# Retention attention and gated convolution: steps of 256 tokens with two tokens per partition instead of steps of 128

## Chip, cores, metric

One core of one Trainium2 chip. The metric is the device time of one execution in microseconds (us). Times are medians of all runs of a kernel. A run counts as slow when it is over 1.5% above the fastest of the same kernel; ratios leave such runs out. On one core this goes by time alone. "Span" is the profiled execution on the core alone, some 2 us shorter than its time.

## The reference

```python
# q, k, v: (B=8, H=8, S=576, D=64) float32; d_model = H*D = 512; conv kernel of 5
scores = q @ k.T / sqrt(D)
gamma  = 1 - 2 ** (-5 - arange(H))
ret    = scores * where(i >= j, gamma ** (i - j), 0)     # causal decay, per head
x      = (ret @ v).transpose(0, 2, 1, 3).reshape(B, S, 512)
gate   = sigmoid(sum_k conv_w[k] * x_padded[:, k:k+S])   # causal depthwise convolution
out    = (gate * (x @ w_val)) @ w_out
```

The decay factors into gamma^i for q and gamma^-j for k. So attention runs in chunks: scores inside a chunk with a 0/1 mask, and a 64x64 state per head for all earlier tokens.

## The kernel before

A step is 128 tokens of one batch (four steps, then one rest step of 64 tokens for two batches together). GpSimd (POOL) casts and scales, TensorE (PE) transposes, VectorE (DVE) and ScalarE (ACT) take the results out of PSUM. The convolution is 160 matmuls of 32x32 tiles in one piece of "fill" work, which stands between attention steps along with the two matrix products.

```python
def load(s):                                  # 256 B per run: one token of one head
    eng.dma_start(out=dst, in_=src[b, :, c*P:(c+1)*P, :].rearrange("h p d -> p h d"))

def scores(s):                                # 64x128 tiles
    for hh in range(2):
        for hp in range(HP):
            nc.tensor.matmul(sc[:, hp, :], lhsT=kt[sl, hp, :], rhs=qt[sl, hp, :], ...)

def state(s):                                 # summed in PSUM, 128x128 matmuls, half of it unused
    for hp in range(HP):
        nc.tensor.matmul(sp[:, hp, :], lhsT=kb[:, 2*hp:2*hp+2, :], rhs=vb[:, 2*hp:2*hp+2, :],
                         start=(c == 0 and hp == 0), ...)
    # ... diagonal blocks copied to w by ScalarE

def attn_out(s):
    # ... o (one PSUM bank): 8 matmuls of 128x64 tiles, 4 from the state
    nc.scalar.copy(xt[:, :, bb, PAD + c*P:PAD + (c+1)*P], o)

for s in range(NS):
    load(s + 4); cast(s + 2); transp(s + 1)
    scores(s); state(s)
    # two pieces of fill (conv, val or outp)
    attn_out(s)
    # one or two pieces of fill
    # at the end of a batch: push_block(...) puts conv, four val, m outp on the list of fill
```

Of the kernel before, what the change touches and what calls it, by code (L numbers as in the profile page):

```python
# [14 lines left out]
F32 = mybir.dt.float32  # L15
# [10 lines left out]

@with_exitstack
def kernel(
# [10 lines left out]
    nc = tc.nc  # L39
# [3 lines left out]
    NC = S // P  # L43
    REM = S - NC * P
# [4 lines left out]
    assert D == 64 and DM == H * D and 2 * REM == P and B % 2 == 0  # L49
# [7 lines left out]
    ld = ctx.enter_context(tc.tile_pool(name="ld", bufs=6))  # L57
    cs = ctx.enter_context(tc.tile_pool(name="cs", bufs=4))
    at = ctx.enter_context(tc.tile_pool(name="at", bufs=3))
    xp = ctx.enter_context(tc.tile_pool(name="xp", bufs=2))  # L60
# [5 lines left out]
    opp = ctx.enter_context(tc.tile_pool(name="opp", bufs=1, space=PS))  # L66
    stp = ctx.enter_context(tc.tile_pool(name="stp", bufs=1, space=PS))
    glp = ctx.enter_context(tc.tile_pool(name="glp", bufs=4, space=PS))


    ident = cst.tile([P, P], BF16)
    make_identity(nc, ident)
    pos_i = cst.tile([P, NC + 1], I32)
    nc.gpsimd.iota(pos_i, pattern=[[P, NC + 1]], base=0, channel_multiplier=1)
    pos = cst.tile([P, NC + 1], F32)
    nc.vector.tensor_copy(pos, pos_i)
    nc.vector.tensor_scalar(pos[REM:P, NC:NC + 1], pos[REM:P, NC:NC + 1], -float(REM), None,
                            op0=ALU.add)
    fq = cst.tile([P, NC + 1, H], F32)
    fk = cst.tile([P, NC + 1, H], F32)  # L80
    for h in range(H):
        nc.scalar.activation(fq[:, :, h], pos, AF.Exp, scale=lng[h])
        nc.scalar.activation(fk[:, :, h], pos, AF.Exp, scale=-lng[h])
    nc.vector.tensor_scalar_mul(fq, fq, scale)

    mask_c = cst.tile([P, P], F32)
    nc.vector.memset(mask_c, 1.0)
    nc.gpsimd.affine_select(mask_c, mask_c, pattern=[[1, P]], base=0, channel_multiplier=-1,
                            compare_op=ALU.is_ge, fill=0.0)
    mask_r = cst.tile([P, P], F32)  # L90
    nc.vector.memset(mask_r, 0.0)
    for half in range(2):
        sl = slice(half * REM, (half + 1) * REM)
        nc.vector.tensor_copy(mask_r[sl, sl], mask_c[sl, sl])


    NW = 4
    wst = []
    for i in range(NW):
        w = cst.tile([P, HP, P], BF16, tag=f"wst{i}")  # L100
        nc.vector.memset(w, 0.0)
        wst.append(w)
# [9 lines left out]
    diag = cst.tile([P, 2, KC, DT, Q], BF16)  # L112
    wval = cst.tile([P, DT, NQ, P], BF16)
    wout = cst.tile([P, NQ, DM], BF16)

    def load_weights():
# [4 lines left out]
        wtmp = cst.tile([P, DT, DM], BF16)  # L121
        nc.gpsimd.dma_start(out=wtmp, in_=moe_w_val.rearrange("(do di) dp -> di do dp", di=P))
        for do in range(DT):
            nc.vector.tensor_copy(wval[:, do].rearrange("p r (c x) -> p r c x", x=Q),
                                  wtmp[:, do].rearrange("p (c r x) -> p r c x", r=NQ, x=Q))
# [5 lines left out]
        nc.vector.tensor_copy(cwh, cw)  # L131
        nc.vector.tensor_tensor(cwl, cw, cwh, op=ALU.subtract)
        nc.vector.tensor_tensor(idr, ident[:, 0:Q], ident[:, Q:2 * Q], op=ALU.add)
        for i in range(2, NQ):
            nc.vector.tensor_tensor(idr, idr, ident[:, i * Q:(i + 1) * Q], op=ALU.add)
        shp = [P, KC * DT, Q]
        for p2, w in ((0, cwh), (1, cwl)):
            nc.vector.tensor_tensor(
                diag[:, p2].rearrange("p k c x -> p (k c) x"),
                idr.unsqueeze(1).to_broadcast(shp),  # L140
                w.rearrange("p k c -> p (k c)").unsqueeze(2).to_broadcast(shp), op=ALU.mult)


    steps = []
    for u in range(B // 2):
        for bb in range(2):
            for c in range(NC):
                steps.append((u, bb, c))
        steps.append((u, None, NC))

    st = {}

    def load(s):
        u, bb, c = steps[s]
        r = st.setdefault(s, {})
        qf = ld.tile([P, H, D], F32)
        kf = ld.tile([P, H, D], F32)
        vf = ld.tile([P, H, D], F32)
        if bb is None:
            for x in range(2):  # L160
                b = 2 * u + x
                sl = slice(x * REM, (x + 1) * REM)
                for dst, src, eng in ((qf, q, nc.sync), (kf, k, nc.sync), (vf, v, nc.sync)):
                    eng.dma_start(out=dst[sl], in_=src[b, :, NC * P:S, :].rearrange("h p d -> p h d"))
        else:
            b = 2 * u + bb
            for dst, src, eng in ((qf, q, nc.sync), (kf, k, nc.sync), (vf, v, nc.sync)):
                eng.dma_start(out=dst, in_=src[b, :, c * P:(c + 1) * P, :].rearrange("h p d -> p h d"))
        r.update(qf=qf, kf=kf, vf=vf)

    def cast(s):
        c = steps[s][2]
        r = st[s]
        qb = cs.tile([P, H, D], BF16)
        kb = cs.tile([P, H, D], BF16)
        nc.gpsimd.tensor_tensor(qb, r["qf"], fq[:, c, :].unsqueeze(2).to_broadcast([P, H, D]), op=ALU.mult)  # L176
        nc.gpsimd.tensor_tensor(kb, r["kf"], fk[:, c, :].unsqueeze(2).to_broadcast([P, H, D]), op=ALU.mult)  # L177
        vb = cs.tile([P, H, D], BF16)
        nc.gpsimd.tensor_copy(vb, r["vf"])  # L179
        r.update(qb=qb, kb=kb, vb=vb)  # L180

    def transp(s):
        r = st[s]
        tp = glp.tile([P, 2, HP, P], BF16, tag="gps", name="tp")
        for n, src in ((0, r["qb"]), (1, r["kb"])):
            for hp in range(HP):
                nc.tensor.transpose(tp[:, n, hp, :], src[:, 2 * hp:2 * hp + 2, :].rearrange("p a d -> p (a d)"), ident)  # L187
        qt = at.tile([P, HP, P], BF16)
        kt = at.tile([P, HP, P], BF16)
        nc.vector.tensor_copy(qt, tp[:, 0])  # L190
        nc.scalar.copy(kt, tp[:, 1])  # L191
        r.update(qt=qt, kt=kt)

    def scores(s):
        u, bb, c = steps[s]
        r = st[s]
        mk = mask_r if bb is None else mask_c
        r["am"] = []
        for hh in range(2):
            sl = slice(hh * D, (hh + 1) * D)  # L200
            sc = scp.tile([P, HP, P], F32)
            for hp in range(HP):
                nc.tensor.matmul(sc[:, hp, :], lhsT=r["kt"][sl, hp, :], rhs=r["qt"][sl, hp, :],  # L203
                                 start=(hp == 0), stop=True, skip_group_check=True)
            am = at.tile([P, HP, P], BF16, tag=f"am{hh}")
            nc.vector.tensor_tensor(am, sc, mk.unsqueeze(1).to_broadcast([P, HP, P]), op=ALU.mult)  # L206
            r["am"].append(am)

    wcur = {}
    wcount = [0]  # L210
    stbank = {}

    def state(s):
        u, bb, c = steps[s]
        if bb is None:
            return
        r = st[s]
        if c == 0:
            stbank[0] = stp.tile([P, HP, P], F32, name="sts")
        sp = stbank[0]  # L220
        for hp in range(HP):
            nc.tensor.matmul(sp[:, hp, :], lhsT=r["kb"][:, 2 * hp:2 * hp + 2, :].rearrange("p a d -> p (a d)"),  # L222
                             rhs=r["vb"][:, 2 * hp:2 * hp + 2, :].rearrange("p a d -> p (a d)"),
                             start=(c == 0 and hp == 0), stop=True, skip_group_check=True)

        w = wst[2 + bb] if c == NC - 1 else wst[c % 2]
        for hh in range(2):
            sl = slice(hh * D, (hh + 1) * D)
            nc.scalar.copy(w[sl, :, hh * D:(hh + 1) * D], sp[sl, :, hh * D:(hh + 1) * D])  # L229
        wcur[(u, bb, c + 1)] = w  # L230
# [3 lines left out]
    def attn_out(s):  # L234
        u, bb, c = steps[s]
        r = st[s]
        if u not in xts:
            xt = xp.tile([P, DT, 2, PAD + S], BF16, name="xt")
            nc.gpsimd.memset(xt[:, :, :, 0:PAD], 0.0)
            xts[u] = xt  # L240
        xt = xts[u]
        o = opp.tile([P, HP, P], F32)
        for hp in range(HP):
            for hh in range(2):
                sl = slice(hh * D, (hh + 1) * D)
                nc.tensor.matmul(o[sl, hp, :], lhsT=r["vb"][:, 2 * hp + hh, :], rhs=r["am"][hh][:, hp, :],  # L246
                                 start=(hp == 0), stop=True, skip_group_check=True)
        if c > 0:
            for hp in range(HP):
                if bb is None:  # L250
                    for x in range(2):
                        cl = slice(x * REM, (x + 1) * REM)
                        nc.tensor.matmul(o[:, hp, cl], lhsT=wcur[(u, x, NC)][:, hp, :], rhs=r["qt"][:, hp, cl],
                                         start=False, stop=True, skip_group_check=True)
# [143 lines left out]
```

## Time and profile before

| | before |
|---|---|
| time, runs beside the changed kernel | 221.05 us (220.55 to 222.78, 4 runs) |
| span of the profiled run | 217.4 us |
| PE busy | 174.5 us |
| PE idle | 42.9 us |
| first scores | 23.10 us |
| first convolution starts; runs through from | 39.12 us; 41.83 us |
| PE idle after 41.83 us | 21.4 us |

PE's busy time comes from the page, idle is span less busy, and the last row is the sum of the windows' lengths less PE's busy time in them. The start, on PE's timeline (37 of the first convolution's 160 matmuls run ahead of 41.83):

```profile
23.10 0.62 PE L203 MATMUL sc<-qt,kt 64*128 64x128 bf16 x8
...
39.12 1.04 PE L288 MATMUL cps<-xt,diag 32*32 32x512 bf16 x15
...
40.62 0.63 PE L288 MATMUL cps<-xt,diag 32*32 32x512 bf16 x22
41.83 2.40 PE L288 MATMUL cps<-xt,diag 32*32 32x512 bf16 x123 [0.57 <-ACT kt L191]
```

Next is the page's list of DMA queues of the kernel before (packets, MB, share of 16 engines' time):

```profile
q1 hardware_dynamic: 117760, 37.76, 79.1%
...
q8 instruction: 27, 0.44, 0.9%
```

The last is PE's waits in the kernel before (us in total, times, longest):

```profile
PE cps L288 <- issue: 5.6, 3, 2.8
...
PE vps L303 <- ACT gt L295: 2.4, 3, 1.6
...
PE cps L288 <- ACT kt L191: 1.2, 4, 0.6
PE cps L288 <- ACT xt L261: 0.7, 2, 0.3
```

Waits are given as us in total, times, longest; "issue" means that PE waits for nothing that the profile shows.

### The profile page before, as it was taken

The page shows a single profiled execution, that of the slowest core. Times are in us where ns is not written, and L with a number is a line of the kernel's source. Part 1 is how long each engine was busy: PE and PEld are TensorE (multiplying, and loading weights), DVE is VectorE, ACT ScalarE, POOL GpSimd, SP SyncE. Part 2 cuts the span into 40 slices and gives each one's busy share as a digit, 9 for nine tenths or more (in the row PEclk, how much of TensorE's full clock was granted, in tenths as well). Part 3 has the DMA queues.
Part 4 walks back from the last instruction along what each step waited for, and adds up shares of the span by engine and source line. Part 5 has one row for each costly group of instructions (what it writes and reads, how often), then busy time and mean ns, then how long its engine had stood idle before and what let it go on. Part 6 is the DMA issues. An engine that isn't in the chain of part 4 may idle for free.

```text
span 217.4 us, 8277 instructions
## 1 busy us (share of the span) xinstructions
PE 174.5 (80%) x3532; PEld 110.5 (51%) x3552; DVE 92.4 (43%) x182; ACT 106.7 (49%) x242; POOL 98.7 (45%) x125
## 2 busy tenths in 40 slices
PE   0003899899949949999999879699898999999950
PEld 0002466455735528665664566356644866576640
DVE  2037434364604415555535255356363454535310
ACT  2021263556803625746863547448457474666321
POOL 7007997471445415708444854355656463200000
PEclk9999999999997996999999999999999999999997
DMA  6999999953998399669899998699989996130122
GB/s 119 177 214 217 217 221 201 183 104 102 275 205 191 106 238 202 135 155 234 245 238 192 218 306 179 156 195 250 289 192 199 236 262 134 58 141 34 69 100 50
DMA packets 121540, 39.33 MB, mean 181 GB/s; under 512 B 115872, under 2 KB 116896, under 8 KB 121504
## 3 DMA queue, kind: packets, MB, share of 16 engines
q1 hardware_dynamic: 117760, 37.76, 79.1%
q0 software_dynamic: 1104, 1.05, 3.0%
q8 instruction: 27, 0.44, 0.9%
q10 hardware_dynamic: 2640, 0.01, 0.7%
q14 instruction: 9, 0.07, 0.1%
HBM read 30.42 MB, written 9.44 MB: 183 GB/s over the span
## 4 chain that ended last, share of the span: by engine, by line
PE 71%; issue 13%; ACT 7%; POOL 5%; DVE 2%; ACTq 0%; POOLq 0%
PE vps L303 15%; PE ops L313 13%; PE cps L288 13%; PE o L246 8%; PE tp L187 8%; PE sc L203 5%; PE sts L222 4%; PE o L256 4%; ACT kt L191 2%; DVE qt L190 2%; ACT w L229 2%; ACT gt L295 2%; POOL qb L176 1%; POOL kb L177 1%; ACT ob L316 1%
## 5 line engine op out<-in xcount | busy, mean ns | idle before, releaser
L176 POOL TENSOR_TENSOR qb<-qf,fq 128x512 bf16<-128x512 f32 x36 | 37.6, 1045 | 67.9 <-DMA qf<-in_q_dram 41.4
L206 DVE TENSOR_TENSOR am<-sc,mask_c 128x512 bf16<-128x512 f32 x64 | 41.8, 683 | 20.8 <-PE sc L203 20.4
L308 DVE TENSOR_TENSOR zt<-gt,vps 128x512 bf16<-128x512 f32 (+2 forms) x52 | 26.8, 523 | 46.8 <-PE vps L303 40.5
L303 PE MATMUL vps<-xt,wval 128*128 128x512 bf16 (+2 forms) x201 | 37.3, 321 | 4.9 <-ACT gt L295 2.4
L177 POOL TENSOR_TENSOR kb<-kf,fk 128x512 bf16<-128x512 f32 x36 | 37.5, 1042 | 6.5 <-DMA kf<-in_k_dram 5.6
L288 PE MATMUL cps<-xt,diag 32*32 32x512 bf16 (+2 forms) x2080 | 31.0, 315 | 9.9 <-issue 5.6
L313 PE MATMUL ops<-wout,zt 128*128 128x512 bf16 x131 | 35.0, 380 | 0.8 <-issue 0.2
L191 ACT COPY kt<-tp 128x512 bf16<-128x512 bf16 x36 | 21.1, 585 | 26.4 <-DVE qt L190 26.2
L295 ACT ACTIVATE gt<-cps 128x512 f32<-128x512 f32 (+2 forms) x52 | 20.0, 471 | 26.9 <-PE cps L288 26.9
L187 PE MATMUL tp<-ident,qb 128*128 128x128 bf16 x144 | 16.0, 237 | 19.6 <-POOL qb L176 19.6
L288 PEld LDWEIGHTS <-diag 32*32 32x32 bf16 x2080 | 22.9, 88 | 16.8 <-issue 14.7
L190 DVE COPY qt<-tp 128x512 bf16<-128x512 bf16 x36 | 15.2, 423 | 37.4 <-PE tp L187 37.2
L229 ACT CAST w<-sts 64x256 bf16<-64x256 f32 x64 | 23.5, 367 | 13.8 <-PE sts L222 13.1
L316 ACT COPY ob<-ops 128x512 f32<-128x512 f32 x36 | 21.1, 586 | 17.1 <-PE ops L313 13.3
L179 POOL CAST vb<-vf 128x512 bf16<-128x512 f32 x36 | 22.0, 610 | 9.8 <-DMA vf<-in_v_dram 5.7
L303 PEld LDWEIGHTS <-wval 128*128 128x128 bf16 x208 | 18.0, 102 | 15.6 <-issue 4.9
L187 PEld LDWEIGHTS <-qb 128*128 128x128 bf16 x144 | 10.9, 105 | 24.0 <-POOL qb L176 20.0
L261 ACT CAST xt<-o 128x512 bf16<-128x512 f32 x32 | 18.9, 591 | 8.2 <-PE o L256 7.8
L246 PE MATMUL o<-am,vb 128*64 128x128 bf16 x288 | 21.1, 239 | 0.2
L203 PE MATMUL sc<-qt,kt 64*128 64x128 bf16 x288 | 20.4, 233 | 0.0
L313 PEld LDWEIGHTS <-zt 128*128 128x128 bf16 x144 | 13.0, 98 | 14.3 <-issue 1.5
L246 PEld LDWEIGHTS <-vb 128*64 128x64 bf16 x288 | 11.8, 115 | 13.7 <-issue 9.5
(40 smaller groups left out, 106.4 us busy)
## 6 DMA issues: line engine op xcount, KB each, us to landing
qf<-in_q_dram SPq DMA_DIRECT2D x32, 256.0 KB, 5.1
kf<-in_k_dram SPq DMA_DIRECT2D x32, 256.0 KB, 5.2
vf<-in_v_dram SPq DMA_DIRECT2D x32, 256.0 KB, 5.6
out_dram<-ob SPq DMA_DIRECT2D x32, 256.0 KB, 2.6
qf<-in_q_dram SPq DMA_DIRECT2D x8, 128.0 KB, 4.3
kf<-in_k_dram SPq DMA_DIRECT2D x8, 128.0 KB, 4.3
vf<-in_v_dram SPq DMA_DIRECT2D x8, 128.0 KB, 4.5
out_dram<-ob SPq DMA_DIRECT2D x8, 128.0 KB, 3.9
```

The lines of the kernel that those rows point to most:

```text
L176: nc.gpsimd.tensor_tensor(qb, r["qf"], fq[:, c, :].unsqueeze(2).to_broadcast([P, H, D]), op=ALU.mult)
L177: nc.gpsimd.tensor_tensor(kb, r["kf"], fk[:, c, :].unsqueeze(2).to_broadcast([P, H, D]), op=ALU.mult)
L187: nc.tensor.transpose(tp[:, n, hp, :], src[:, 2 * hp:2 * hp + 2, :].rearrange("p a d -> p (a d)"), ident)
L191: nc.scalar.copy(kt, tp[:, 1])
L203: nc.tensor.matmul(sc[:, hp, :], lhsT=r["kt"][sl, hp, :], rhs=r["qt"][sl, hp, :], start=(hp == 0), stop=True, skip_group_check=True)
L206: nc.vector.tensor_tensor(am, sc, mk.unsqueeze(1).to_broadcast([P, HP, P]), op=ALU.mult)
L229: nc.scalar.copy(w[sl, :, hh * D:(hh + 1) * D], sp[sl, :, hh * D:(hh + 1) * D])
L246: nc.tensor.matmul(o[sl, hp, :], lhsT=r["vb"][:, 2 * hp + hh, :], rhs=r["am"][hh][:, hp, :], start=(hp == 0), stop=True, skip_group_check= ...
L288: nc.tensor.matmul(cps[r][c * Q:(c + 1) * Q], lhsT=diag[rs, p2, kk, c, :], rhs=win(c, kk)[rs], start=(kk == 0 and p2 == 0), stop=(kk == KC ...
L303: nc.tensor.matmul(vp, lhsT=wval[:, do, d, :], rhs=win(do, PAD), start=(do == 0), stop=(do == DT - 1))
L308: nc.vector.tensor_tensor(zv, g[d], vp, op=ALU.mult)
L313: nc.tensor.matmul(op, lhsT=z[0][:, d, m * P:(m + 1) * P], rhs=wout[:, d, :], start=(d == 0), stop=(d == DT - 1))
```

## The change

Its intent: 512 B runs for the loads, 64x64 matmul tiles (four at a time) without unused halves, a state that takes no PSUM bank for itself, and the attention constants ahead of the weights, so that attention starts earlier. A step becomes 256 tokens with tokens 2p and 2p+1 in partition p. The core of the diff:

```diff
 def load(s):
-    eng.dma_start(out=dst, in_=src[b, :, c*P:(c+1)*P, :].rearrange("h p d -> p h d"))
+    nc.sync.dma_start(out=t.rearrange("p h r d -> p h (r d)"),
+        in_=src[2*u+bb, :, n*SC:(n+1)*SC, :].rearrange("h (p r) d -> p h (r d)", r=R))
+load(0)
+# positions, factors, masks here; weights' transfers now after cast(0), their copies in prep_weights()
 def transp(s):                      # one bank for k and one for q, 8 transposes each
 def scores(s, hps):                 # half of the head pairs per call
-    nc.tensor.matmul(sc[:, hp, :], lhsT=kt[sl, hp, :], rhs=qt[sl, hp, :], ...)
+    nc.tensor.matmul(sc[hh][HS[x], a, rj, :], lhsT=kt[HS[hh], hp, rj, HS[x]],
+                     rhs=qt[HS[hh], hp, :, HS[x]], ...)
 def state(s, x):                    # twice per step
+    nc.tensor.matmul(ds[HS[hh], hp, :], lhsT=kb[HS[x], rr, h, :], rhs=vb[HS[x], rr, h, :], ...)
+    nc.vector.tensor_tensor(sn, ds, scur[(u, bb)], op=ALU.add)
 def attn_out(s, hps, lastg):        # two o banks, both taken out at the end of the step
+    for x in range(2):
+        nc.scalar.copy(xt[:, :, bb, t0:t0+P].rearrange("p a (i r) -> p a r i", r=R), o[x]...)
 # loop
-    load(s + 4)
+    load(s + 3)
+    # large step: fill(1) scores(ga) state(0) fill(2) scores(gb) attn_out(ga) fill(2)
+    #             state(1) attn_out(gb) fill(2)
```

## The prediction

> **What bounds the kernel now.** I read the page's summary first, then the waits, the start of the timeline, and at last TensorE's own timeline.
>
> ```profile
> PE 174.5 (80%) x3532; PEld 110.5 (51%) x3552; DVE 92.4 (43%) x182; ACT 106.7 (49%) x242; POOL 98.7 (45%) x125
> PE 71%; issue 13%; ACT 7%; POOL 5%; DVE 2%; ACTq 0%; POOLq 0%
> ```
>
> TensorE (PE) is the only engine near full, and 71% of the chain that ended last is PE. The 20% of the 217.4 us that PE is not busy lies mostly at the start. The waits say why:
>
> ```profile
> POOL qb L176 <- DVE fq L84: 12.9, 1, 12.9
> DVE cwh L131 <- DMA qf<-in_q_dram: 12.0, 1, 12.0
> ...
> ACT fq L82 <- DVE pos L77: 10.0, 1, 10.0
> ```
>
> and the first 18 us of the timeline give the order:
>
> ```profile
> 14.28 0.18 DVE L131 CAST cwh<-cw 128x20 bf16<-128x20 f32 x1 [11.97 <-DMA qf<-in_q_dram]
> ...
> 14.86 0.15 DVE L77 TENSOR_SCALAR pos<-pos 64x1 f32<-64x1 f32 x1
> ...
> 17.36 0.18 DVE L84 TENSOR_SCALAR fq<-fq 128x40 f32<-128x40 f32 x1
> ...
> 17.62 1.21 POOL L176 TENSOR_TENSOR qb<-qf,fq 128x512 bf16<-128x512 f32 x1 [12.92 <-DVE fq L84]
> ```
>
> The positions that the decay factors need stand on DVE behind a cast of the convolution weights, which waits for its transfer until 14.28. So the first q cast starts at 17.62, though its data had long landed. After that, PE runs attention alone until the first convolution (39.12), at half speed: compare the cold lines with those of 150 us.
>
> ```profile
> 37.39 0.61 PE L256 MATMUL o<-qt,w 128*128 128x128 bf16 x4
> 37.93 0.62 PE L203 MATMUL sc<-qt,kt 64*128 64x128 bf16 x7
> ...
> 149.13 0.41 PE L246 MATMUL o<-am,vb 128*64 128x128 bf16 x8
> 149.48 0.40 PE L256 MATMUL o<-qt,w 128*128 128x128 bf16 x4
> 149.71 0.39 PE L187 MATMUL tp<-ident,qb 128*128 128x128 bf16 x4
> 149.94 0.39 PE L187 MATMUL tp<-ident,kb 128*128 128x128 bf16 x4
> 150.25 0.41 PE L203 MATMUL sc<-qt,kt 64*128 64x128 bf16 x8
> 150.59 0.40 PE L222 MATMUL sts<-vb,kb 128*128 128x128 bf16 x4
> 150.83 0.39 PE L187 MATMUL tp<-ident,qb 128*128 128x128 bf16 x4
> ```
>
> Starts count here, not durations, since matmuls overlap. Start to start: four full-array N=128 matmuls in 0.54 us cold, 0.23 warm; eight sc in 0.34, eight o in 0.35, warm. In the windows by pair of batches PE is nearly full:
>
> ```profile
> 41.83:90.97 49.14, 42.75 (x805) 26.89 (x810) 20.64 (x39) 26.19 (x55) 23.69 (x28) 0.93 0.79 177
> 90.97:134.30 43.33, 40.06 (x839) 25.39 (x844) 21.09 (x40) 25.43 (x56) 21.13 (x25) 1.00 0.96 216
> 134.30:178.19 43.89, 40.19 (x840) 25.30 (x845) 20.89 (x40) 25.33 (x56) 25.63 (x31) 1.00 0.94 223
> ```
>
> The first pair takes 5.5 us more than the next two; in it PE stops inside a convolution, waiting for no engine:
>
> ```profile
> 64.08 0.73 PE L288 MATMUL cps<-xt,diag 32*32 32x512 bf16 x26 [2.83 <-issue]
> ...
> 80.96 0.29 PE L288 MATMUL cps<-xt,diag 32*32 32x128 bf16 x18 [2.23 <-issue]
> ```
>
> After the first stop the next N=512 matmuls run at 0.43 us instead of 0.22 for some 3 us: cold again.
>
> Transfers are the second bound. At 20 to 30 us only the q, k, v loads run, in 256 B pieces: 218 GB/s, 8632 packets at 131% of 16 engines' 10 us, so 24 ns each. The pairs at 90 to 178 us move 216 to 223 GB/s, the same rate. POOL waits 41.4 us for qf in all, but PE waits for POOL only at the start (18.9 of 19.6 us), so this bound lies just behind PE.
>
> **What the Trainium skill says.** (1) "DMA: Bandwidth & Descriptors", Specifications: transfers need at least 512 B for line rate; below, the engines read, modify and write. This trace has only the slow side, 218 GB/s at 256 B. (2) "Runtime: NRT & Kernel Launch", Instruction fetch mechanics: instructions are streamed in 16 KiB blocks of 256 by DMA. The trace agrees: the instruction queue moved 27 packets, 0.44 MB, and PE's 7084 instructions are 27.7 such blocks. That the two stops above are late blocks behind queued loads is my inference. (3) "TensorEngine Tiling (Array Packing)", Restrictions: column tiling disables fast weight load; Key Properties: a change of tiling mode drains the array. The trace agrees: o, alternating two 128x64 tiles of N=128 (53 ns at full clock), goes at 0.35/8 = 43 ns each instead of 27. So one tile repeats every 86 ns: 53 of stream and some 33 of load that is not hidden. Changes of mode cost some 0.08 us (tp to sc: 0.54 us for eight at 0.056). (4) "TensorE: Matmul & The Clock Gate", Part 1: full clock only after some 3.4 us of activity. The trace is slower to agree: PE stayed cold through 14 us of nearly unbroken attention work and was warm only once the convolution ran (41.83).
>
> **The change part by part.**
>
> *Start.* Loads of the first step go first, then positions and factors, weights behind. Sixteen exponentials 0.1 us apart after the 1.28 us table load end by about 4 to 7 us. The first loads (2 x 512 KB at an estimated 300 GB/s plus 2 us) are in by 5 to 7. So POOL starts at about 6 instead of 17.62. But a step is twice as large: casts of 2 x 1.045 twice, plus 1.2, are 5.4 us, and PE's first scores stand behind the second step's transposes: 6 + 5.4 + 4.2 + about 2 for issuing weight transfers is 17.5. Two steps follow at the cold clock. Per step, doubling the warm figures below: transposes 1.8, scores 1.4, state 1.9, o 1.4, state's product 0.9, about 7 us. So the first convolution comes at about 32 against 39: **minus 7 us**.
>
> *PE in the steady stage.* Per 256 tokens before: 2 x (8 tp 0.45, sc 0.34, sts 0.21, o 0.34, o from state 0.21) = 3.1 us. After: 16 tp 0.9; 32 sc in four 64x64 tiles, one per 86/4 = 21.5 ns: 0.69; 32 o likewise 0.69; 32 state matmuls of N=64, only two tiles at a time since one row half is used per call: (27 + 33)/2 = 30 ns, 0.96; 8 from state 0.45. Sum 3.7, **0.6 more**. The four 64x64 tiles don't pay, since before the two-tile forms overlapped too, and the state costs double. Mode changes fall from 8 to about 6 (minus 0.15). The four rest steps gain 0.3 each. Over the 14 steps behind the start: 14 x 0.45 - 1.2 = **plus 5 us**. PE matmuls rise from 3552 to 4512 (tp 288, sc 576, state 512, o 576 + 128, the rest as before), about 35 instruction blocks.
>
> *Transfers.* Input packets halve from 110,592 to 55,296. At 24 to 30 ns each the load queue's share falls from 79% to some 40 to 50%. No PE time follows directly, but the late instruction blocks should go: the excess of the first pair, 5.5 us, of which I take three quarters, **minus 4 us**.
>
> *DVE and ACT.* State sums add 32 x 0.42 (zt of the same 128x256 shape took 0.422) = 13.4 us to DVE; larger q copies save 16 x 0.15 and smaller masks of the rest steps 8 x 0.26: 92 becomes about 101. ACT saves some 2.5 in k copies. Both stay under half. But each state now goes PE, DVE 0.42, ACT 2 x 0.37 before the o of the same step, about 2.6 us behind the scores counting the two masks ahead of it (1.37). With fill of two pieces (1.7) and the next scores (0.35) between, it just fits; in the half of the steps that run short of fill it does not. I take **plus 2 us**. The two o banks and one bank per transpose take waits away: **minus 2 us**. POOL stays about 98. The tail after the last o is the same 11 pieces of work: 0.
>
> Sum: -7 + 5 - 4 + 2 - 2 = -6, so a span of 211.4; with the 3.2 us between span and median, about **214.5 us**. With the prior that a change so much worked on removes some waits that I can't see, I put 213.5.
>
> **Rivals.**
> - *The transfer bound is the real one.* 216 to 223 GB/s in the steady pairs equals the saturated rate, which speaks for it; that PE never waits for POOL after the start speaks against. If it holds, pairs shrink from 43.6 towards PE's own 38 us and the time is about 200.
> - *The smaller matmuls become the cost.* If tiles don't overlap as o's do, or the added 27% of instructions stall fetching, add 0.5 us per 256 tokens and stops: 220 to 226. For: a convolution of N=128 matmuls already goes at 8.7 ns apiece where the array would allow under 5, and stops follow it. Against: at 21.5 ns apiece attention is far from that.
> - *The start is not shortened.* Engines don't follow source order (line 131 before line 76 on DVE), so DVE or POOL may again stand behind a weight transfer. Then only the other terms count: about 220.
>
> **Range and chances.** The start is worth 3 to 11 us, the steady PE term 0 to +10, the fetch term 0 to -6, waits -5 to +6. Combined, 205 to 221. Faster than 216.2 (2%) is rather likely, since the start's mechanism is plain: 0.62; within 2%: 0.28; slower: 0.10.
>
> **What would show it.** Right: first POOL cast at about 6, first cps at about 32, sc and o at about 21 ns start to start, state at 30 ns, loads over 280 GB/s while saturated, first pair no longer than the others. Wrong: a pair under 40 us (the transfers bound it), sc above 30 ns, a first cast later than 12, or new waits of PE for DVE sn or ACT w over 5 us in all.

## The result, and the profile after

246.6 us (245.71 to 247.72, 4 runs) against 221.05: **11% slower**, ratio 1.1143 with a 95% interval of 1.1063 to 1.1223. All ratios here are the mean time of one kernel's fast runs over that of the kernel before in the same rounds, so not quite the ratio of the medians. The experiments ran on several chips, and some medians hold slow runs, so kernels are compared by their ratios: a difference of 0.01 between two ratios is 2.2 us.

The page of the changed kernel, busy time and DMA queues:

```profile
PE 172.3 (70%) x4489; PEld 111.2 (45%) x4512; DVE 108.4 (44%) x198; ACT 112.1 (46%) x230; POOL 92.6 (38%) x83
...
q1 hardware_dynamic: 67840, 37.76, 59.1%
...
q8 instruction: 35, 0.57, 1.0%
```

PE is busy 2.2 us less than before and the loads take 20 points less of the DMA time, as they should. Still the span is 27.2 us longer: PE idles 72.3 us instead of 42.9. PE's waits in the changed kernel say on what:

```profile
PE cps L336 <- issue: 10.6, 5, 4.3
PE sc L231 <- DVE qt L211: 10.5, 1, 10.5
PE cps L336 <- ACT xt L308: 7.2, 7, 1.1
PE o L292 <- ACT wst L268: 2.9, 9, 0.6
PE cps L336 <- ACT kt L213: 2.3, 6, 0.5
```

Three things, then: one long wait at the start, stops on "issue", and hand-overs from ACT that were hardly there before.

**The start.** DVE's timeline of the changed kernel, then PE's first scores:

```profile
10.57 0.86 DVE L164 CAST cwh<-cw 128x20 bf16<-128x20 f32 x1 [7.66 <-DMA cw<-in_moe_conv_w_dram]
...
20.52 8.34 DVE L173 COPY wval<-wtmp 128x512 bf16<-128x512 bf16 x4 [4.60 <-DMA wtmp<-in_moe_w_val_dram]
28.78 0.68 DVE L211 COPY qt<-tpq 128x1024 bf16<-128x1024 bf16 x1
```

```profile
29.51 0.64 PE L231 MATMUL sc<-qt,kt 64*64 64x128 bf16 x16 [10.51 <-DVE qt L211]
```

DVE executes in its own order, and the scheduler again put weights ahead of attention: a cast that waits for the convolution weights until 10.57 stands before the positions, and four copies of the value weights stand before the first qt. Those copies wait for their transfer until 20.52, and then take 8.34 us. The transfer was late because GpSimd issued it behind its first cast, of v, which waited for its load until 10.36. GpSimd's timeline, before and after:

```profile
1.61 0.94 POOL L122 DMA_DIRECT2D wtmp<-in_moe_w_val_dram  x1
```

```profile
11.34 0.94 POOL L153 DMA_DIRECT2D wtmp<-in_moe_w_val_dram  x1
```

In the kernel before the same four copies took 2.6 us. The groups of instructions, before and after (busy time, mean ns of one):

```profile
L124 DVE COPY wval<-wtmp 128x512 bf16<-128x512 bf16 x4 | 2.6, 708 | 0.0
```

```profile
L173 DVE COPY wval<-wtmp 128x512 bf16<-128x512 bf16 x4 | 8.3, 2143 | 4.6 <-DMA wtmp<-in_moe_w_val_dram 4.6
```

The means hide two kinds of copy. The same instructions again (ns, shortest, median and longest):

```profile
L124 DVE COPY wval<-wtmp x4: 286/707/1132, 17.4 to 18.9; 128x512 bf16<-128x512 bf16 x4
```

```profile
L173 DVE COPY wval<-wtmp x4: 1615/1986/2986, 20.5 to 26.9; 128x512 bf16<-128x512 bf16 x4
```

In the kernel before, two copies are done within 0.3 us of the start of GpSimd's first cast (17.62), at 0.29 us each; the other two, beside casts of 1.1 to 1.2 us, take 1.13. In the changed kernel all four stand beside casts. The Trainium skill, "SBUF — State Buffer", section "SBUF: two separate sides", says that DVE in its fast copy mode and GpSimd take turns on one pair of ports, each for a whole instruction. The trace agrees: GpSimd casts without a pause from 20.06 to 29.7 us, its casts of q and k now take 1.9 us instead of 1.03, since a step has twice the size, and each copy ends 0.14 to 0.18 us after one of these casts does. The second copy lets two casts pass (1.96 and 1.03 us) and takes 2.99. First scores come at 29.51 us instead of 23.10.

**Hand-overs.** A convolution of the changed kernel, on PE's timeline:

```profile
102.03 0.59 PE L336 MATMUL cps<-xt,diag 32*32 32x512 bf16 x13 [1.10 <-ACT xt L308]
...
102.90 2.18 PE L336 MATMUL cps<-xt,diag 32*32 32x512 bf16 x131 [0.28 <-ACT kt L213]
```

A step's whole o is now taken out at its end, in two ACT casts of 750 ns (591 before, one at a time), and the next step's kt copy (1019 ns for 256 tokens) queues beside them. ACT's casts of o, before and after:

```profile
L261 ACT CAST xt<-o 128x512 bf16<-128x512 f32 x32 | 18.9, 591 | 8.2 <-PE o L256 7.8
```

```profile
L308 ACT CAST xt<-o 128x512 bf16<-128x512 f32 x32 | 22.4, 750 | 34.1 <-PE o L284 33.7
```

The convolution comes first after that. It does not read kt. By the program it needs all four banks of its pool, and the transposed k holds one until its copy is done; that its wait for kt is a wait for this bank is my reading. The larger step bunches what was spread before. PE's waits for other engines after 45 us (the gaps over 0.15 us, which the profiler names, summed over its timeline) rise from 6.1 to 20.1 us.

**Stops on issue.** They sum to 16.6 us after the start, 9.1 in the kernel before. One more belongs to the latter: its wait of 1.60 us at 139.01 is put down to ACT gt, but by the count of weight loads, which is complete in every trace, it stands where such stops fall (experiment 2). With it, the kernel before has 10.7 us of stops and 4.5 of waits. Two stops of the changed kernel:

```profile
76.39 0.61 PE L336 MATMUL cps<-xt,diag 32*32 32x512 bf16 x2 [4.26 <-issue]
...
144.54 0.26 PE L336 MATMUL cps<-xt,diag 32*32 32x128 bf16 x10 [2.79 <-issue]
```

Some stops are followed by some microseconds at half clock. Windows of the changed kernel show it, behind a stop of 1.88 us that ended at 51.15, and for the first and the third pair of batches (length, then PE, weight loads, DVE, ACT and POOL busy with counts, then PE's clock, DMA share, GB/s):

```profile
53.00:55.00 2.00, 2.00 (x5) 0.74 (x5) 0.69 (x1) 0.58 (x2) 0.90 (x1) 0.50 1.17 294
```

```profile
45.25:102.90 57.65, 44.87 (x1082) 27.62 (x1087) 22.36 (x42) 28.24 (x53) 27.29 (x22) 0.88 0.91 229
...
154.62:201.49 46.87, 39.48 (x1080) 25.76 (x1085) 23.11 (x43) 26.73 (x52) 11.75 (x8) 1.00 0.24 75
```

The same work took 44.87 us of PE in the first pair at a mean clock of 0.88, and 39.48 in the third at full clock.

**The account.** Up to the convolution that runs through, 45.25 us instead of 41.83: +3.4. After it, idle 42.1 us instead of 21.4: +20.7. The two sums give nearly that: stops +5.9, waits +14.6 (without the 1.0 us right ahead of 45.25). PE busy after it 157.3 instead of 154.15: +3.1, half clock included. 3.4 + 20.7 + 3.1 = 27.2 us, the whole difference. Cut at the first matmul of a convolution (39.12 in the kernel before), the same parts are +6.1, +20.2 and +1.0: the start costs 3.4 to 6.1 us, as one counts.

**The matmuls were not the cost.** PE's timeline near the end, at full clock and without loads:

```profile
215.39 0.42 PE L231 MATMUL sc<-qt,kt 64*64 64x128 bf16 x16
215.64 0.42 PE L255 MATMUL ds<-vb,kb 64*64 64x64 bf16 x16
215.99 0.82 PE L361 MATMUL ops<-wout,zt 128*128 128x512 bf16 x2
```

Start to start, 16 score matmuls take 0.25 us with the change of mode behind them, 16 of the state 0.35.

### The profile page after: what moved, and what is told of

Read it like the earlier page. It is cut to its first block, busy times and chain, and to the rows that moved or that the text cites. A ratio compares the mean times of both kernels' runs of the same rounds, so it can differ in the third digit from the quotient of the medians.

```text
span 244.6 us, 9940 instructions
## 1 busy us (share of the span) xinstructions
PE 172.3 (70%) x4489; PEld 111.2 (45%) x4512; DVE 108.4 (44%) x198; ACT 112.1 (46%) x230; POOL 92.6 (38%) x83
## 3 DMA queue, kind: packets, MB, share of 16 engines
q1 hardware_dynamic: 67840, 37.76, 59.1%
## 5 line engine op out<-in xcount | busy, mean ns | idle before, releaser
L194 POOL TENSOR_TENSOR kb<-kf,fk 128x1024 bf16<-128x1024 f32 (+1 forms) x20 | 35.0, 1751 | 54.3 <-PE ds L255 45.4
L194 POOL TENSOR_TENSOR qb<-qf,fq 128x1024 bf16<-128x1024 f32 (+1 forms) x20 | 34.7, 1736 | 32.3 <-PE tpq L207 17.0
L268 ACT CAST wst<-sn 64x256 bf16<-64x256 f32 x64 | 25.8, 403 | 18.2 <-DVE sn L265 13.2
L343 ACT ACTIVATE gt<-cps 128x512 f32<-128x512 f32 (+2 forms) x52 | 20.1, 472 | 30.1 <-PE cps L336 30.1
L231 PE MATMUL sc<-qt,kt 64*64 64x128 bf16 (+1 forms) x576 | 21.0, 229 | 14.4 <-DVE qt L211 10.5
L231 PEld LDWEIGHTS <-kt 64*64 64x64 bf16 x576 | 12.8, 110 | 26.8 <-issue 24.6
L213 ACT COPY kt<-tpk 128x1024 bf16<-128x1024 bf16 (+1 forms) x20 | 18.8, 939 | 11.3 <-PE tpk L207 11.2
L196 POOL CAST vb<-vf 128x1024 bf16<-128x1024 f32 (+1 forms) x20 | 19.1, 954 | 12.2 <-DMA vf<-in_v_dram 12.2
L207 PE MATMUL tpk<-ident,kb 128*128 128x128 bf16 x144 | 12.6, 233 | 15.2 <-POOL kb L194 15.2
L284 PE MATMUL o<-am,vb 64*64 64x128 bf16 (+1 forms) x576 | 21.8, 224 | 2.2 <-issue 1.1
L211 DVE COPY qt<-tpq 128x1024 bf16<-128x1024 bf16 (+1 forms) x20 | 12.7, 637 | 20.4 <-PE tpq L207 20.0
L361 PEld LDWEIGHTS <-zt 128*128 128x128 bf16 x144 | 12.8, 97 | 13.8 <-issue 2.5
L207 PEld LDWEIGHTS <-kb 128*128 128x128 bf16 x144 | 10.0, 105 | 17.3 <-POOL kb L194 15.2
```

Of the source, the lines that this page charges most:

```text
L194: nc.gpsimd.tensor_tensor(dst, src.rearrange("p h r d -> p r h d"), f[:, f0:f0 + R, :].unsqueeze(3).to_broadcast(shp), op=ALU.mult)
L207: nc.tensor.transpose(tp[:, hp, rr, :], src[:, rr, 2 * hp:2 * hp + 2, :].rearrange("p a d -> p (a d)"), ident)
L231: nc.tensor.matmul(sc[hh][HS[x], a, rj, :].rearrange("p (r i) -> p r i", r=R), lhsT=r["kt"][HS[hh], hp, rj, HS[x]], rhs=r["qt"][HS[hh], hp ...
L268: nc.scalar.copy(w[HS[hh], :, hh, :], sn[HS[hh]])
L284: nc.tensor.matmul(o[x][HS[hh], hp, :], lhsT=r["vb"][HS[x], rj, 2 * hp + hh, :], rhs=r[("am", hps[0], hh)][HS[x], a, rj, :], start=(hp == ...
L361: nc.tensor.matmul(op, lhsT=z[0][:, d, m * P:(m + 1) * P], rhs=wout[:, d, :], start=(d == 0), stop=(d == DT - 1))
```

## The experiments

Thirteen kernels ran, one of them twice. All but the three "noload" kernels compute the right result. Line numbers differ from kernel to kernel.

### 1. Loads taken away, from both kernels

```diff
 def load(s):
+    if s > 4 or s == 3:            # changed kernel; s > 3 and s != 8 in the kernel before
+        r[nm] = held[...][nm]      # tiles of an earlier step, no transfer
+        return
```

> The changed kernel, with loads only for the first three large steps and the first rest step; later steps cast the same tiles again, so the result is wrong on purpose. PE's instruction order is the same row for row. Theory 1 (blocks of 256 PE instructions arrive late, and later the more the loads fill the DMA engines; after a long stop PE is cold for 3.4 us or more): the stops of 1.9, 4.3 and 2.8 us shrink to about 1.2 us as in the unloaded tail, the cold stretches after them go, pairs 1 and 2 (57.7 and 51.7 us) come down to about the 47 us of pair 3, and with a shorter start the time is about 228 us (224 to 233). Theory 2 (the new hand-overs between engines are the loss, loads have nothing to do with it): only the start gains, 238 to 244 us.

> The kernel before with the same removal of loads, wrong on purpose. Theory 1: the stops of 2.8 and 2.2 us in its first pair shrink to about 1 us and the pair falls from 49.1 to about 44 us; about 212 us. Theory 2: as before but for the start, 217 to 220 us. The difference between the changed kernel and this one without loads is what does not come from the loads: about 16 us by theory 1 (3 us per pair, 4 in the tail, some at the start), about 25 by theory 2.

Measured: 235.46 us (ratio 1.0576) and 206.39 us (ratio 0.9355). Without loads the stops fall to 7.7 and 5.2 us (2.7 by the profile's labels, and two put down to other engines, see experiment 2), but the ratios stay 0.122 apart (27 us), as they were with loads (0.114, 25 us). The changed kernel's waits for other engines after 45 us stand at 20.0 us and its wait for qt at 10.5, as with loads. So contention with the loads makes each kernel slower by some 12 to 14 us and is not what separates them. (The first steps' loads stayed in both, so this says nothing of the start.) My figure for the theory of stops, a gap of some 16 us, missed.

### 2. 128 dummy instructions ahead of the changed kernel

```diff
+    for _ in range(64):
+        nc.tensor.matmul(padt[:, 0:Q], lhsT=ident, rhs=ident[:, 0:Q], start=True, stop=True)
     transp(0)
```

> The changed kernel with 64 small matmuls (128 PE instructions) ahead of its first transpose, where PE is idle anyway; all other instructions and their order are the same. Theory 1: the stops move to other instructions, half a block of 256 further on, so that their sum changes (16 us of issue stops now; I can't say which way: 236 to 256 us, and not within 0.5% of 246.6). If the stops have nothing to do with blocks of instructions, they stay at the same matmuls and the time stays within 0.5%.

Measured: 243.69 us, ratio 1.1081 (1.0952 to 1.1211), not to be told from the changed kernel, so the forecast that the time would change is not confirmed. The stops moved: none at the places of the changed kernel, instead 3.46 us at 82.48, 2.94 at 118.97, 2.80 at 147.09, 2.60 at 184.28 and 2.58 at 214.13. Their sum, 15.2 us, hardly changed. Where PE stops is thus a matter of an instruction's number, not of what it is. Counting PE's records (weight loads, matmuls and the few of its sequencer) in the traces in which none is missing, the long stops come before numbers 961, 1729, 2497, 4545 and 6081 in one kernel (a_sxlo, below) and 1729, 3521, 4033 and 7105 in another (b_noload): all 193 plus a multiple of 256. Those before 4033 (0.99 us) and 7105 (1.57 us) the profile puts down to ACT and DVE. In the eight other full traces (both padded kernels among them) every stop on issue after 45 us stands at the same place in its block. The instruction queue moved 35 packets of 16 KB, one for 256 instructions. So I read them as late blocks of instructions. A convolution is 320 instructions in about 2.4 us; that it runs through a block faster than the next one arrives fits, but no run measured the fetch by itself.

### 3. 256 B runs in the new layout

```diff
-    nc.sync.dma_start(out=t..., in_=src[...].rearrange("h (p r) d -> p h (r d)", r=R))
+    for rr in range(R):
+        nc.sync.dma_start(out=t[:, :, rr, :], in_=src[...].rearrange("h (p r) d -> r p h d", r=R)[rr])
```

> The changed kernel with the same layout but loads in runs of 256 B (twice the DMAs of half the size). The engines' orders change in some places. If the 512 B runs, by filling the queues with twice the bytes, are what delays the instruction blocks, the time comes down by 5 us or more. By theory 1 alone loads of 256 B occupy the DMA engines longer, so the stops last at least as long over more of the run: 245 to 255 us, with loads at about 215 GB/s against 260 to 280.

Measured: 242.41 us, ratio 1.0814 (interval 1.0633 to 1.0996). Slower loads did not make it slower; the stops sum to 18.0 us. But the start changed as well: in this build GpSimd issued the value weights' transfer at 2.97 us instead of 11.34. DVE's timeline:

```profile
13.57 3.46 DVE L174 COPY wval<-wtmp 128x512 bf16<-128x512 bf16 x4
16.96 0.68 DVE L212 COPY qt<-tpq 128x1024 bf16<-128x1024 bf16 x1
```

The copies still stand ahead of the first qt, yet first scores come at 17.69 us: DVE's order alone does not make the late start; the late transfer and the copies beside GpSimd belong to it. The first convolution comes at 40.57, 4.7 us earlier than in the changed kernel. So this run does not measure the runs' length alone. It does not show any gain from 512 B runs.

### 4. The start repaired

```diff
+    load_weights()                 # transfers issued ahead of the first casts
     cast(0)
-    load_weights()
 # cast(), first step:
+    nc.gpsimd.tensor_copy(vb[:, 0, 0, 0:1], qb[...])      # holds v's cast behind q's
 # prep_weights(), now called behind the first scores:
+    nc.vector.tensor_copy(cwh[:, 0, 0:1], am[...])        # holds the diagonals behind am
-    nc.vector.tensor_copy(wval[:, do]..., wtmp[:, do]...)
+    nc.scalar.copy(wval[:, do, 0, 0:1], kt[...])          # holds the copies behind kt(0)
+    nc.scalar.copy(wval[:, do]..., wtmp[:, do]...)
```

(A one-column copy from a later tile is what keeps the scheduler from moving the work ahead.)

> The changed kernel with only the order at the start altered: weight transfers issued before the first casts on GpSimd, the value-weight copies moved to ScalarE behind kt(0), the diagonals behind the first mask product, so that VectorE's first qt copy stands behind no weight transfer. Theory 'the start is a third of the loss' (first sc comes at 29.5 us because qt stood behind the value-weight copies, before: 23.1): first sc at about 17, first large convolution at about 35 instead of 45.3, time about 237 (ratio to before 1.07), pairs as in the changed kernel. Rival 'the start is paid for anyway, since PE then waits for the second step's loads': first sc early, but first convolution at 42 or later and time above 243.

Measured: 240.15 us, ratio 1.0825, about 7 us better. First scores came at 22.07 instead of 29.51, not at 17: the second step's kb waits for its k load until 17.17 us. The copies on ACT took 0.61 to 0.62 us each, so it was DVE, beside GpSimd, that made them 2.1. The run changes four things at once (transfers, v's cast, copies, diagonals) and does not tell their shares. Part of the gain was lost again later: at 94.03 us a convolution waits 4.6 us for xt, behind a rest step whose q and v loads came late (GpSimd waits 13.6 us for q). Both theories were half right.

### 5. The xt cast split between ACT and DVE

```diff
-    nc.scalar.copy(xt[...], o[x]...)
+    cp = nc.scalar.copy if x == 0 else nc.vector.tensor_copy
+    cp(xt[...], o[x]...)
```

> The changed kernel with the cast of the second 128 tokens of o (xt) on VectorE instead of ScalarE, nothing else. Theory 'hand-overs': the seven waits of PE for ScalarE xt of 1.0 to 1.1 us before a convolution (7.2 us in all) shrink to about 0.4, and with kt coming earlier its waits too; time about 241 (5 us less). Rival 'the waits only show where the time goes, instruction blocks or half clock set it': the sum of waits falls, issue stops grow, time within 2 us of 246.

Measured: 238.06 us, ratio 1.0717, about 9 us better, and more than expected. PE's waits in this kernel:

```profile
PE cps L337 <- ACT xt L309: 3.2, 6, 0.7
```

The sum of waits for other engines fell from 20.1 to 11.9 us, the stops rose by 2.3. Moving 16 casts to another engine gives back a third of the loss. The hand-overs are real, not a shadow of something else.

### 6. Fewer instructions for the state

```diff
-    for hh in range(2):
-        nc.tensor.matmul(ds[HS[hh], hp, :], lhsT=kb[HS[x], rr, h, :], rhs=vb[HS[x], rr, h, :], ...)
+    nc.tensor.matmul(ds[:, hp, :], lhsT=kb[HS[x], rr, 2*hp:2*hp+2, :], rhs=vb[HS[x], rr, 2*hp:2*hp+2, :], ...)
+    # VectorE adds the two diagonal blocks
```

> The changed kernel with the state's increments taken as 128x128 products (the diagonal 64x64 blocks are used) instead of pairs of 64x64: 256 matmuls and 512 instructions fewer on PE, two instruction blocks less, though the array's time for the state is not less (8 of 53 ns instead of 16 of 21 ns), and VectorE adds in two halves. Theory 'instructions': two stops less, and fewer of those in the short conv steps; time about 242 (4 us less). Rival 'the array's time counts': time 247 or more.

Measured: 247.64 us, ratio 1.1076 with an interval of 1.0932 to 1.122: no gain that can be told from zero. The page says why:

```profile
PE 182.7 (74%) x4236; PEld 120.0 (49%) x4256; DVE 122.7 (50%) x230; ACT 111.7 (46%) x230; POOL 92.7 (38%) x83
```

The stops did halve, from 16.6 to 8.5 us, but PE is busy 10.4 us more. Both theories came true at once and cancel. Eight of these matmuls take 0.55 us start to start, the sixteen small ones 0.35: over 32 calls 6.4 of the 10.4 us. So the small tiles are cheaper for the array than this form, and their price is instructions. The full-array form of the kernel before is cheaper still: 0.48 us for 256 tokens (four matmuls in 0.24, in the prediction's lines), against 0.70.

### 7. The start repaired in the kernel before

```diff
 # load_weights(): transfers only; prep_weights() behind the first scores, as in 4
+    nc.vector.tensor_copy(cwh[:, 0, 0:1], am[...])
+    nc.scalar.copy(wval[:, do, 0, 0:1], kt[...])
+    nc.scalar.copy(wval[:, do]..., wtmp[:, do]...)
```

> The kernel before with only the order of its start altered as in a_start2: positions and factors ahead of the weights' casts, value-weight copies on ScalarE behind kt(0), diagonals behind the first mask product. Theory: the prediction's start term was right for what it described (first POOL cast at about 7 instead of 17.6, first sc at about 14 instead of 23.1), and would have come out in the kernel before: first convolution at about 34 instead of 41.8, time about 214 (7 us less than before). Rival: the loads of the next steps or the cold clock hold the first convolution at 40 or later, time above 218.

Measured: 215.59 us with two fast and two slow runs, ratio of the fast ones 0.963. GpSimd's first cast starts at 6.94 us instead of 17.62, and the first scores at 17.28 instead of 23.10 (its profile is of a slow run; the fast one of the repeat has 6.94 and 17.72). This version is **faster than both kernels**.

> b_start2 once more with five rounds, since only two of its four runs were of the fast state: 213.5, ratio 0.963, if it stands; 219 or more if its gain was chance.

Measured: 212.76 to 214.17 us in three fast runs, 217.31 to 220.1 in three that count as slow; ratio 0.9697 (0.9636 to 0.9758). It stands. But half of its ten runs count as slow, against 3 of 11 of the kernel before in the last rounds, with no lower clock (0.973 to 0.980 in the repeat): by the medians of all runs, 215.74 to 220.69, the gain is 2.2%.

### 8. Both repairs in the changed kernel

The diffs of 4 and 5 together.

> The changed kernel with both repairs at once: the start's order of a_start2 and the split xt cast of a_xt. Theory 'the loss is a sum of separate parts: start about 6, hand-overs about 8': the two gains add, 246.6 - 6.5 - 8.5 = about 231.5 (ratio to before 1.045). Rival 'with both, the loads or the instruction blocks take back what is won': 236 or more, with the wait of GpSimd for the q load of a rest step (13.6 us in a_start2) or issue stops over 20 us.

Measured: 236.2 us, ratio 1.0727. The rival was right: not better than the split cast alone (1.0717), so the gains do not add. At 92.51 us a convolution waits 2.87 us for xt, again behind late loads. The other half of the rival, stops over 20 us, did not come: they sum to 13.8.

### 9. Loads further ahead, convolution later

```diff
-    load(s + LOOK + 1)             # three load buffers
+    load(s + LOOK + 2)             # four for large steps, two for rest steps
-    fill(1); scores(s, ga); state(s, 0); fill(2)
+    scores(s, ga); state(s, 0); fill(3)       # where the next fill is a convolution
```

> As a_sx, and the loads one step further ahead (four load buffers instead of three for the large steps, two for the rest steps), and a convolution pushed at the end of a step begins behind the scores and the state product of the next step instead of right behind its transposes. Theory: late loads and the wait of the convolution for xt and kt are what keeps a_sx from the kernel before; both go, about 226 (5 less than a_sx), what is left being issue stops, about 15 us against 9 in the kernel before. Rival 'issue stops and the half clock behind them carry it': within 2 us of a_sx.

Measured: 230.59 us, ratio 1.0435, about 6 us better than a_sx and well off the expected 226. Stops 11.5 us, waits 13.2. GpSimd's waits:

```profile
POOL kb L197 <- DMA kf<-in_k_dram: 33.7, 6, 14.1
```

Its transfers now run at 203 to 295 GB/s from 12 us all the way to about 108 us. The same kernel without loads shows what that costs:

> a_sxlo with q, k and v loaded for the first steps only (wrong on purpose), PE order unchanged row for row. Theory 'after the repairs the first half of the changed kernel is bound by its transfers': GpSimd's waits for loads (33.7 us for k) and the wait of PE at 90.7 us go, third pair unchanged; time about 219 (11 less than a_sxlo). Rival 'what remains is PE's own: hand-overs and block fetches without contention': at most 5 us less than a_sxlo, 225 or more. In the kernel before the same edit gave 206.4, 14 less.

```profile
POOL kb L203 <- DMA kf<-in_k_dram: 6.7, 1, 6.7
```

Measured: 218.83 us, ratio 0.9933: 11 us less, as the theory of transfers said. That they bind the first half is not shown by this: the same edit took 12 to 14 us off the two unrepaired kernels, and in a_sxlo PE waits for GpSimd only once after the start, 2.4 us at 90.73. The rest of the 11 us are stops (11.5 to 6.6) and PE's busy time (177.3 to 171.8, at a mean clock of 0.94, and of 0.96 in the profiled run without loads). So the loads seem to cost mostly through late instructions and half clock. The 12 us left to b_noload (206.39) are PE's: waits 10.7 against 4.8 us, stops 6.6 against 5.2, PE busy 171.8 against 168.9, and the start.

### 10. Is the kernel before lucky in its blocks?

The 64 dummy matmuls of 2, in the kernel before.

> The kernel before with 64 small dummy matmuls (128 PE instructions) at its start, in the time in which PE waits for its first operands: nothing else changes on any engine, only the place of every instruction in its 256-instruction block. Theory 'more instructions are what costs in the changed kernel, the alignment is chance': stops move to other instructions, their sum stays near 9 us, time within 2% of before. Rival 'the kernel before is lucky in its alignment, the changed one not': sum of stops 14 us or more, time 226 or more.

Measured: 222.24 us, ratio 1.0062 (0.9904 to 1.0219). The stops moved and sum to 12.1 us instead of 10.7 (9.1 by the labels), the time is the same within some 1.6%. Here another alignment gave 1.4 us more of stops and no more time that can be told. What the changed kernel has more of is blocks, 35 against 27.

### 11. Weights behind the first loads, in the kernel before

```diff
+    nc.gpsimd.tensor_copy(wtmp[:, 0, 0:1], vb1[...])   # holds the transfer behind the second step's cast
     nc.gpsimd.dma_start(out=wtmp, ...)
+    nc.gpsimd.tensor_copy(vb[:, 0, 0:1], kb[:, 0, 0:1])  # first step: holds v's cast behind k's
 # prep_weights() now behind the third step's scores
```

> b_start2 with the value and output weights' transfers issued behind the casts of the second step instead of at the start, and their copies behind the third step's kt. Theory 'in b_start2 the start is bound by transfers, nine steps' loads and the weights at 218 GB/s, wherever the weights stand': first sc at about 13 instead of 17.3, but the first convolution within 1.5 us of b_start2's 35.4 and the time within 1% of b_start2. Rival 'the wait for the first v load (4.4 us) is what counts': first convolution at about 31, 4 us less in all.

PE's timeline of this kernel:

```profile
12.70 0.62 PE L212 MATMUL sc<-qt,kt 64*128 64x128 bf16 x8
...
35.60 2.40 PE L297 MATMUL cps<-xt,diag 32*32 32x512 bf16 x145 [0.98 <-ACT kt L200]
```

The first scores come 5 us earlier than in b_start2, at 12.70 us, and the convolution runs from 35.60 all the same (35.22 in the repeated b_start2): PE then waits 3.7 us at 26.25 for a cast whose load is late. 215.92 us in all with only two fast runs (211.47 and 211.79; the profile is of a slow one), ratio 0.9611 (0.954 to 0.9682), within 1% of b_start2. The two kernels move 198 to 223 GB/s from 10 to 36 us, about the 218 of the kernel before, so a start bound by transfers wherever the weights stand is the better reading. As v's cast was moved too, the run does not separate the two.

## Why the prediction was wrong

Predicted 213.5 us (205 to 221), measured 246.6. By its own steps:

- **"Minus 7 us" for the start: failed.** It took the source order for the order of execution. The third rival named this ("DVE or POOL may again stand behind a weight transfer"), but gave it "about 220" as if that only set the term to zero. In fact the first scores came 6.4 us later than before and the first convolution at 45.25 us, not 32 (39.12 before): the value weights' transfer was issued at 11.34 us instead of 1.61, and their four copies, ahead of the first qt, took 8.34 us beside GpSimd instead of 2.6. Experiment 7 shows that the mechanism as such was right: done so that the scheduler keeps to it, it takes 3 to 4% off the kernel before (fast runs).
- **"Plus 2 us, minus 2 us" for waits: the step that failed most.** I looked at the state's way through DVE and ACT, which costs 2.9 us in all, and not at the larger hand-over at the end of each step, xt and kt ahead of a convolution. Waits rose by 14.6 us. Nor did "one bank per transpose" take waits away: the convolution now waits 2.3 us for kt (1.2 before), as I read it for the bank that this frees. The range of "minus 5 to plus 6" did not hold it. Experiment 5 takes about 9 us back with one line.
- **"Minus 4 us" for late instruction blocks: wrong sign.** I took late loads as the cause of the stops. Shorter transfers did not cure them: 35 blocks instead of 27 go by, and attention, as I read it, uses up instructions faster. Stops rose by 5.9 us. That contention makes the stops longer was right (experiment 1: from 16.6 to 7.7 us in all).
- **"Plus 5 us" for PE's own work: too pessimistic, and harmless.** Sixteen scores took 0.25 us, so 32 take 0.5 instead of 0.69, and 32 state matmuls 0.70 instead of 0.96. The 64x64 tiles pay for the scores (0.50 us for 256 tokens, 0.68 before) and not for the state (0.70, 0.48 before; the sum took 0.21 for each of its two halves where its own lines give 0.24). PE was busy 2.2 us less in all, in spite of more time at half clock.
- **Transfers: right in direction, short in size.** The share fell to 59.1%, not to "40 to 50%". The sum halves all input packets, but the rest steps keep their 256 B runs: the load queue, with the outputs, lost 49,920 packets and not 55,296. And a packet now takes 34 ns (59.1% of 16 engines' 244.6 us for 67,840), above the "24 to 30". The rival "the transfer bound is the real one" was wrong for the change. In the mended kernels PE waits for late loads at single places (2.4 to 4.6 us, experiments 4, 8 and 9), no more.
- **"What would show it wrong"** named a first cast later than 12 us (v was cast at 10.36, k, which PE waited for, at 12.92) and new waits for ACT w or DVE sn. It missed xt and kt.

So the start and the waits failed by their mechanism: the order in which engines run, and the work that stands behind a step's end. How the 27.2 us divide over causes is settled to the extent of the account above. The single repairs give 7 and 9 us but do not add, so a figure for each cause by itself is not to be had. I have not found out what part of the stops more instructions cause by themselves, apart from their spacing: the one kernel with fewer of them also changed PE's work.

## What to carry to other kernels

A larger step saves fixed costs and bunches hand-overs: look at what stands first behind the end of a step, and give its inputs to two engines or put other work between. A reordering at the start counts only where the engine's own order shows it. Count instructions per microsecond as well as matmul time: a stretch that runs through 256 instructions in about 2 us, as a convolution does here, may stop at a block's edge, wherever that falls.

## What the Trainium skill lacked or had wrong

- "Runtime: NRT & Kernel Launch", Instruction fetch mechanics, calls the cost of crossing a block "mostly hidden". On PE here it is not hidden at every edge: stops of up to 4.3 us, always at the same place in a block of 256 (193 plus a multiple), 10.7 us in all in the kernel before and 16.6 after, and 5.2 and 7.7 where the loads are gone.
- "SBUF — State Buffer", SBUF: two separate sides, has the lock right; the runs add what it costs. A 128x512 copy on DVE takes 0.29 us alone, 1.13 beside GpSimd casts of 1.1 to 1.2 us, and 1.6 to 3.0 beside casts of up to 1.96, the longest after two casts in a row had gone first. On ACT it takes 0.6 us.
- "TensorE: Matmul & The Clock Gate", Why this matters for your kernels, advises no gaps of PE over some 3 us. Here a stop of 1.88 us that ended at 51.15 (with 0.57 us of idle time just before 49.0) was followed by over 6 us at a clock of 0.50, while one of 2.79 us at 144.54 was followed by 2.5 us at 1.00: the length of the gap alone doesn't tell.
